# Weight blocks read into the place of their own low parts, a first operand made ahead, and two pools exchanged

## The chip, the cores and the metric

The kernel runs on one core of one Trainium2 chip. The time is device microseconds of one launch. In the core five engines work side by side, each through its own instructions in order: TensorE (PE) multiplies matrices, VectorE (DVE) and ScalarE (ACT) work element by element, GpSimd (POOL) does little here, and SyncE (SP) issues nearly all DMA transfers, one after another. Engines wait for each other through semaphores: an instruction that waits holds everything behind it on its engine.

## What is computed

Attention with a capped score, then two blocks of matrix products (shapes: 4 x 12 heads x 448 x 64, so 1792 tokens of 768; inner width 1024), all in float32:

```python
scores = cap * np.tanh(scale * np.matmul(q, k.transpose(0, 1, 3, 2)) / cap)
attn = softmax(scores)                       # with 1e-9 added to the sum
x = heads side by side of np.matmul(attn, v) # 1792 x 768
h = ((x @ w1) * (x @ w2)) @ w3 @ w_out       # first block, 1792 x 768
h = h @ w_in                                 # second block, 1792 x 1024
solu = h * softmax(h)
ln = (solu - mean) / np.sqrt(var + 1e-6) * g_ln
out = ln @ w_out2                            # 1792 x 768
```

`w3 @ w_out @ w_in` is multiplied into one matrix (`w_dr`) while attention runs, and `g_ln` is multiplied into the last matrix (`wg_dr`).

## The kernel before

A product of two float32 matrices is made of three matmuls (`THREE`): every operand is split into a high part (a cast to float32r, on ACT) and a low part (the rest, a subtraction on DVE). `split(th, tl, x)` does both, at lines 174 and 175, so the trace shows every split at these lines, under the name of the tile that is written.

Three stages follow each other. Attention runs with the products of the weights beside it. Then `gated()` makes `ab = (x @ w1) * (x @ w2)` for 16 steps of `f` (PE line 570; DVE multiplies at 578 into `abs`, and SP stores it to `ab_dr`). Beside it `ahead`, a list of loads and conversions, prepares what comes later. The last stage, which the change touches, multiplies by `w_dr` and by `wg_dr` in pairs of token tiles (128 tokens each, seven pairs). Both sides are cut 2 x 2, and seven products instead of eight are made of sums of the four pieces (`seven`, with operands numbered 1, 2, 6, 7, 5, 4, 3 in the order of use). For these products there are:

- weight blocks `ws[m]` (for `w_dr`) and `wg[m]` (for `wg_dr`), m = 1 to 7, each 128 x 4 x 512 (384 for `wg`) with a high and a low part. Blocks 5, 6, 7, 4 are sums that were made ahead and stored (`tw_dr`, `tg_dr`). `EARLY` blocks 1, 2, 6, 7, 5 of `ws` are loaded by `plan_block` during `gated()`, the `LATE` ones 4 and 3 at the start of the last stage. Every `wg[m]` takes the very place of `ws[m]`, once the last pair's product m has read it.
- operands `a[m]` of a pair (`operands`, or `turned_operands` for `wg`): pieces of the tokens and their sums `s1` to `s4`. The tokens come through landing buffers too: `ldab` (`load_ab`) and `ldc` (`load_c`), two tiles a pair.

There are three landing buffers (`LANDS`, tag `ld`) for all loads of this kind. In the kernel before, half a weight block (`part`) is read into a landing buffer (`landing`), split from there (`block_part`), and the buffer is then free for the next load.

Operands 1 and 2 of the first pair are made ahead of the stage (`first_operands`), in places of the pool `w3p`; operand 6 and the others are made by `operands(0)` after it. At the start of the last stage the pools of `gated()` are closed and `wsl` (late blocks), `hp` (sums, copies of products, `h`, `e`) and `op` (operands) are opened in their place, one behind another. A tile waits for whatever read or wrote its place before.

`solu` works on finished pairs of `h` (DVE and ACT) and stores `e` to `c_dr`. The last pair of `ws` (n = 6) has the first pair of `wg` following; `turned` transposes tokens on PE (line 760, `tp`). The order in which instructions of independent parts stand on an engine is made by a scheduler at build time, so the change also moves instructions that it doesn't name.

Of the kernel before, what the change touches and what calls it, by code (L numbers as in the profile page):

```python
# [10 lines left out]
F32 = mybir.dt.float32  # L11
F32R = mybir.dt.float32r
# [33 lines left out]
def raw(ap):  # L46

    return ap.bitcast(F32)
# [50 lines left out]
def attention_moe_solu(ctx: ExitStack, tc: tile.TileContext, q, k, v, cap, w12, w3t, wo, win, wout2, g_ln, out):  # L99
# [31 lines left out]
    def opened(stack, name, side="left"):  # L131
        cm = tc.tile_pool(name=name, bufs=1, side=side, reuse_waits="tile")
        stack.append(cm)
        return cm.__enter__()
# [15 lines left out]
    def landing(i, src, n, kind):  # L150
        t = conv.tile([P, 2 * HALF], U32, tag="ld", bufs=LANDS, name=f"ld{i}")
        lands[i] = t[:, :n].bitcast(kind)
        dst = lands[i]
        if len(src.shape) == 3:
            dst = dst.rearrange("p (a b) -> p a b", a=src.shape[1])
        elif len(src.shape) == 4:
            dst = dst.rearrange("p (a b c) -> p a b c", a=src.shape[1], b=src.shape[2])
            for g in range(src.shape[1]):
                sync.dma_start(out=dst[:, g], in_=src[:, g])
            return  # L160
        sync.dma_start(out=dst, in_=src)
# [11 lines left out]
    def split(th, tl, x):  # L173
        act.copy(th, x)
        dve.tensor_tensor(tl, x, raw(th), ALU.subtract)  # L175
# [301 lines left out]
    def block_src(m, part, dr, t_dr):  # L477

        two = slice(2 * part, 2 * part + 2)
        if m in (6, 7, 5, 4):  # L480
            return t_dr[(5, 6, 7, 4).index(m), :, two, :]
        g, h = {1: (0, 0), 2: (1, 0), 3: (1, 1)}[m]
        return dr[two, :, g, h, :].rearrange("i p n -> p i n")

    def block_part(i, dst, part):
        x = lands.pop(i)
        two = slice(2 * part, 2 * part + 2)
        split(dst[:, 0, two, :], dst[:, 1, two, :], x.rearrange("p (a n) -> p a n", a=2))

    def fifth(m):  # L490
        if m not in place["ws"]:
            close(right, 1)
            place["w5"] = opened(right, "ws5", "right")
            place["ws"][m] = place["w5"].tile([P, 2, NF // 2, HALF], F32R, tag=f"w{m}", name=f"ws{m}")
        return place["ws"][m]

    def plan_block(m, part):
        i = len(ahead.items)
        there = (lambda: "ws" in place) if m != EARLY[4] else (lambda: (NF + 5, PASSES[1][1]) in fin)
        ahead.add(("f", m, part), lambda: landing(i, block_src(m, part, W4, tw_dr), 2 * HALF, F32), lambda: None,  # L500
                  lambda: block_part(i, fifth(m), part), None, there)

    def plan_last(f):
        for u in range(2):
# [40 lines left out]
    def operand(a, m, x, name, p=None):  # L545
        a[m] = op.tile([P, 2, HALF], F32R, tag="op", bufs=NOP, name=f"{name}_{m}") if p is None else p
        split(a[m][:, 0], a[m][:, 1], x)
# [1 line left out]
    begun = {}  # L549

    def first_operands():
        x = lands["ab0"]
        for m, h in ((1, 0), (2, 1)):
            operand(begun, m, x[:, h * HALF:(h + 1) * HALF], "a0", w3p.tile([P, 2, HALF], F32R, tag="w3", bufs=W3, name=f"a0_{m}"))
    ahead.add("a0", lambda: load_ab(0), lambda: None, first_operands, None, lambda: (NF + 2, PASSES[1][0]) in fin)

    def gated():
# [119 lines left out]

    wsl, hp, op = opened(left, "wsl"), opened(left, "hp"), opened(left, "op")  # L680
    for m in LATE:
        ws[m] = wsl.tile([P, 2, NF // 2, HALF], F32R, tag=f"w{m}", name=f"ws{m}")
    ps_cm = tc.tile_pool(name="ps3", bufs=1, space=PSUM, reuse_waits="tile")
# [36 lines left out]
    def operands(n):  # L720

        x1, x2 = (lands.pop(f"ab{t}") for t in (2 * n, 2 * n + 1))
        a11, a12, a21, a22 = x1[:, :HALF], x1[:, HALF:], x2[:, :HALF], x2[:, HALF:]
        s1, s2, s3, s4 = (hp.tile([P, HALF], F32, tag="sm", bufs=4, name=f"s{i}_{n}") for i in range(4))
        a, name = (dict(begun) if n == 0 else {}), f"a{n}"
        if n:
            operand(a, 1, a11, name)
            operand(a, 2, a12, name)
        dve.tensor_tensor(s1, a21, a22, ALU.add)
        dve.tensor_tensor(s2, s1, a11, ALU.subtract)  # L730
        operand(a, 6, s2, name)
        dve.tensor_tensor(s3, a11, a21, ALU.subtract)
        operand(a, 7, s3, name)
        operand(a, 5, s1, name)
        operand(a, 4, a22, name)
        dve.tensor_tensor(s4, a12, s2, ALU.subtract)
        operand(a, 3, s4, name)
        return a
# [48 lines left out]
    def load_wg(m):  # L787
        wg[m] = (wsp if m in EARLY[:4] else place["w5"] if m in EARLY else wsl).tile([P, 2, NF // 2, HALF], F32R, tag=f"w{m}", name=f"wg{m}")[:, :, :, :w]
        for part in range(2):
            landing("wg", block_src(m, part, G4, tg_dr), 2 * w, F32)  # L790
            block_part("wg", wg[m], part)

    a = operands(0)
    for m in LATE:
        for part in range(2):
            landing("wl", block_src(m, part, W4, tw_dr), 2 * HALF, F32)
            block_part("wl", ws[m], part)
    load_ab(1)
    for n in range(PAIRS):
        tps, last = {}, n + 1 == PAIRS  # L800
        if last:
# [83 lines left out]
```

## Time and profile before

| | us |
|---|---|
| median of 3 runs | 857.79 (857.79 to 859.17) |
| the profiled execution | 857.35 |
| its span, first to last instruction | 854.4 |
| PE busy | 828.9 |
| DVE busy | 598.4 |
| ACT busy | 480.8 |

The span is what the trace's clock counts; 2.95 us of the profiled execution lie around it. PE is busy for 97% of it, with a matmul counted as busy until its modelled end, so that a running series of short ones overlaps.

### The profile page before, as it was taken

The page shows a single profiled execution, that of the slowest core. Times are in us where ns is not written, and L with a number is a line of the kernel's source. Part 1 is how long each engine was busy: PE and PEld are TensorE (multiplying, and loading weights), DVE is VectorE, ACT ScalarE, POOL GpSimd, SP SyncE. Part 2 cuts the span into 40 slices and gives each one's busy share as a digit, 9 for nine tenths or more (in the row PEclk, how much of TensorE's full clock was granted, in tenths as well). Part 3 has the DMA queues.
Part 4 walks back from the last instruction along what each step waited for, and adds up shares of the span by engine and source line. Part 5 has one row for each costly group of instructions (what it writes and reads, how often), then busy time and mean ns, then how long its engine had stood idle before and what let it go on. Part 6 is the DMA issues. An engine that isn't in the chain of part 4 may idle for free.

```text
span 854.4 us, 12340 instructions
## 1 busy us (share of the span) xinstructions
PE 828.9 (97%) x4392; PEld 687.7 (80%) x4392; DVE 598.4 (70%) x1068; ACT 480.8 (56%) x745; POOL 75.3 (9%) x147
## 2 busy tenths in 40 slices
PE   6999999999999999999989999999999999899998
PEld 4677998767677777777778899997788888799998
DVE  7999977887766587777874443444888877974452
ACT  5789538798777576767753112122465565653341
POOL 1011101111101111101101000000000000100000
PEclk8999999999999999999999999999999999899999
DMA  7886785686863376658769799793533234662211
GB/s 267 260 231 196 221 243 160 228 288 210 286 205 91 89 260 213 201 183 289 247 201 314 248 384 385 261 309 121 149 122 99 99 109 151 212 244 105 105 62 74
DMA packets 91549, 173.48 MB, mean 203 GB/s; under 512 B 9696, under 2 KB 61152, under 8 KB 89440
## 3 DMA queue, kind: packets, MB, share of 16 engines
q1 hardware_dynamic: 86496, 161.51, 56.8%
q0 software_dynamic: 4992, 11.19, 5.2%
q8 instruction: 34, 0.56, 0.3%
q14 instruction: 27, 0.22, 0.1%
HBM read 116.40 MB, written 50.68 MB: 196 GB/s over the span
## 4 chain that ended last, share of the span: by engine, by line
PE 45%; DMA 9%; DVE 6%; ACT 4%; issue 3%; POOL 0%; DVEq 0%; POOLq 0%; ACTq 0%
PE ab L570 18%; PE u L693 13%; PE v L693 6%; PE y L693 3%; DMA wg_dr<-cv 3%; PE o L271 2%; DMA rb<-r_dr 1%; PE tp L760 1%; DMA r_dr<-inv 1%; DMA wt<-w_dr 1%; ACT p L240 1%; DVE wg L175 1%; DMA ldwg<-wg_dr 1%; DVE cv L169 1%; DVE cv L170 1%
## 5 line engine op out<-in xcount | busy, mean ns | idle before, releaser
L570 PE MATMUL ab<-xs,wt 128*128 128x448 f32 x1152 | 249.0, 370 | 0.1
L570 PEld LDWEIGHTS ab<-xs,wt 128*128 128x128 f32 x1152 | 215.8, 189 | 27.6 <-issue 8.0
L239 ACT ACTIVATE sc<-sc,qscale 128x896 f32<-128x896 f32 x96 | 83.8, 885 | 34.7 <-PE sc L232 34.2
L271 PE MATMUL o<-hi,v 128*66 128x448 f32 (+1 forms) x396 | 94.4, 369 | 2.0 <-DVE hi L255 1.0
L240 ACT ACTIVATE p<-sc,capt 128x896 f32<-128x896 f32 x96 | 86.7, 920 | 1.1 <-PE o L271 0.3
L693 PE MATMUL u<-ws,a 128*128 128x512 f32 x336 | 81.2, 392 | 3.2 <-ACT u L697 2.0
L255 DVE TENSOR_TENSOR lo<-p,hi 128x896 fp32r<-128x896 f32 x66 | 71.5, 1084 | 13.9 <-ACT hi L251 13.7
L353 PEld LDWEIGHTS f<-w,w_o 128*128 128x128 f32 x576 | 72.6, 191 | 7.9 <-issue 4.1
L353 PE MATMUL f<-w,w_o 128*128 128x256 f32 x576 | 77.8, 288 | 0.0
L693 PEld LDWEIGHTS u<-ws,a 128*128 128x128 f32 x336 | 62.8, 188 | 17.4 <-ACT u L697 2.4
L371 PE MATMUL f<-w_i,w 128*128 128x512 f32 x288 | 74.7, 398 | 1.0 <-DVE w L175 1.0
L693 PE MATMUL u<-wg,c 128*128 128x384 f32 x336 | 66.7, 343 | 1.7 <-DVE wg L175 1.0
L371 PEld LDWEIGHTS f<-w_i,w 128*128 128x128 f32 x288 | 52.8, 188 | 17.2 <-issue 4.0
L271 PEld LDWEIGHTS o<-hi,v 128*66 128x66 f32 (+1 forms) x396 | 44.3, 135 | 24.7 <-DVE hi L255 3.2
L251 ACT CAST hi<-p 128x896 fp32r<-128x896 f32 x66 | 62.6, 950 | 0.5 <-PE o L271 0.4
L693 PEld LDWEIGHTS u<-wg,c 128*128 128x128 f32 x336 | 58.9, 190 | 3.4 <-DVE wg L175 1.8
L574 ACT COPY a<-ab 128x448 f32<-128x448 f32 x32 | 17.1, 533 | 76.1 <-PE ab L570 68.3
L168 DVE TENSOR_SCALAR cv<-ld 128x512 uint32<-128x512 uint32 (+1 forms) x80 | 32.5, 409 | 32.3 <-DMA wg_dr<-cv 13.6
L169 DVE SCALAR_TENSOR_TENSOR cv<-ld,cv 128x512 uint32<-128x512 uint32 (+1 forms) x80 | 52.0, 657 | 0.6
L170 DVE SCALAR_TENSOR_TENSOR cv<-ld,cv 128x512 uint32<-128x512 uint32 (+1 forms) x80 | 51.9, 658 | 0.5
L282 POOL DMA_DIRECT2D xr<-x x48 | 25.6, 535 | 280.4 <-ACT x L281 280.4
L271 PE MATMUL o<-lo,v 128*66 128x448 f32 x132 | 47.4, 365 | 1.1 <-DVE lo L255 1.1
(129 smaller groups left out, 1234.8 us busy)
## 6 DMA issues: line engine op xcount, KB each, us to landing
ld<-in_w SPq DMA_DIRECT2D x24, 512.0 KB, 4.5
w_dr<-wt SPq DMA_DIRECT2D x8, 1536.0 KB, 7.4
wt<-w_dr SPq DMA_DIRECT2D x8, 1536.0 KB, 7.7
ld<-in_w3t SPq DMA_DIRECT2D x16, 512.0 KB, 4.2
ab_dr<-abs SPq DMA_DIRECT2D x32, 224.0 KB, 4.9
ldab<-ab_dr SPq DMA_DIRECT2D x14, 512.0 KB, 3.9
c_dr<-e SPq DMA_DIRECT2D x14, 512.0 KB, 2.8
ldc<-c_dr SPq DMA_DIRECT2D x14, 512.0 KB, 4.4
```

The costliest lines, as they stand in the source:

```text
L168: dve.tensor_scalar(x, hi, 5, 2, ALU.logical_shift_left, ALU.logical_shift_right)
L169: dve.scalar_tensor_tensor(x, hi, 0xC0000000, x, ALU.bitwise_and, ALU.bitwise_or)
L170: dve.scalar_tensor_tensor(x, lo, 29, x, ALU.logical_shift_right, ALU.bitwise_or)
L239: act.activation(sc[:, :w, :S], sc[:, :w, :S], AF.Tanh, scale=qscale)
L240: act.activation(p, sc[:, :w, :S], AF.Exp, scale=capt)
L251: act.copy(hi, p)
L255: dve.tensor_tensor(lo, p, raw(hi), ALU.subtract)
L271: pe.matmul(outs[n, j][:v_.shape[-1], :S], v_, t[rows, j if c < 3 else 0], **flags)
L353: pe.matmul(f[:, :QW], lw[:, a], rw[:, e], start=(g == 0 and m == 0), stop=(g == NF - 1 and m == 2))
L371: pe.matmul(f, w34[:, a, c, :], rw[:, e], start=(c == 0 and m == 0), stop=(c == NC - 1 and m == 2))
L570: pe.matmul(pp[f, b, i][:, :S], w[:, u], xs[b, c][:, e], start=(c == 0 and m == 0), stop=(c == NC - 1 and m == 2))
L693: pe.matmul(bank, a[m][:, x, k * P:(k + 1) * P], wb[m][:, e, k, :], start=(first and k == 0 and i == 0), stop=(k == NF // 2 - 1 and i == 2 ...
```

## The change

A weight block is read by DMA straight into the place of its low part; the split then casts from there into the high part and subtracts in place. `block_load` and `block_split` take the place of `landing` and `block_part`, for early and late `ws` blocks and for `wg`. The two half blocks of a `wg` are loaded one behind the other and then split. Block 5's load stands behind the last sums for `tg_dr`, since its place is opened at the load now. The four loads of late blocks and the second pair's tokens are issued in the code ahead of `operands(0)`. `first_operands` also makes `s1`, `s2` (in the two buffers of tag `cv`) and operand 6 of the first pair. `op` is opened ahead of `hp`.

```diff
@@ -482,10 +482,12 @@
         g, h = {1: (0, 0), 2: (1, 0), 3: (1, 1)}[m]
         return dr[two, :, g, h, :].rearrange("i p n -> p i n")
 
-    def block_part(i, dst, part):
-        x = lands.pop(i)
-        two = slice(2 * part, 2 * part + 2)
-        split(dst[:, 0, two, :], dst[:, 1, two, :], x.rearrange("p (a n) -> p a n", a=2))
+    def block_load(m, part, dr, t_dr, dst):
+        sync.dma_start(out=raw(dst[:, 1, 2 * part:2 * part + 2, :]), in_=block_src(m, part, dr, t_dr))
+
+    def block_split(dst, part):
+        hi, lo = (dst[:, i, 2 * part:2 * part + 2, :] for i in range(2))
+        split(hi, lo, raw(lo))
 
     def fifth(m):
         if m not in place["ws"]:
@@ -495,10 +497,9 @@
         return place["ws"][m]
 
     def plan_block(m, part):
-        i = len(ahead.items)
-        there = (lambda: "ws" in place) if m != EARLY[4] else (lambda: (NF + 5, PASSES[1][1]) in fin)
-        ahead.add(("f", m, part), lambda: landing(i, block_src(m, part, W4, tw_dr), 2 * HALF, F32), lambda: None,
-                  lambda: block_part(i, fifth(m), part), None, there)
+        there = (lambda: "ws" in place) if m != EARLY[4] else (lambda: (NF + 5, PASSES[1][1]) in fin and ("tg", NF // 2 - 1, 1) in ahead.done)
+        ahead.add(("f", m, part), lambda: block_load(m, part, W4, tw_dr, fifth(m)), lambda: None,
+                  lambda: block_split(ws[m], part), None, there)
 
     def plan_last(f):
         for u in range(2):
@@ -549,9 +550,17 @@
     begun = {}
 
     def first_operands():
-        x = lands["ab0"]
-        for m, h in ((1, 0), (2, 1)):
-            operand(begun, m, x[:, h * HALF:(h + 1) * HALF], "a0", w3p.tile([P, 2, HALF], F32R, tag="w3", bufs=W3, name=f"a0_{m}"))
+        x1, x2 = lands["ab0"], lands["ab1"]
+        s1, s2 = first_sums = [conv.tile([P, HALF], U32, tag="cv", bufs=2, name=f"s{i}_0").bitcast(F32) for i in (1, 2)]
+        begun["sums"] = first_sums
+
+        def begin(m, x):
+            operand(begun, m, x, "a0", w3p.tile([P, 2, HALF], F32R, tag="w3", bufs=W3, name=f"a0_{m}"))
+        begin(1, x1[:, :HALF])
+        begin(2, x1[:, HALF:])
+        dve.tensor_tensor(s1, x2[:, :HALF], x2[:, HALF:], ALU.add)
+        dve.tensor_tensor(s2, s1, x1[:, :HALF], ALU.subtract)
+        begin(6, s2)
     ahead.add("a0", lambda: load_ab(0), lambda: None, first_operands, None, lambda: (NF + 2, PASSES[1][0]) in fin)
 
     def gated():
@@ -677,7 +686,7 @@
 
 
 
-    wsl, hp, op = opened(left, "wsl"), opened(left, "hp"), opened(left, "op")
+    wsl, op, hp = opened(left, "wsl"), opened(left, "op"), opened(left, "hp")
     for m in LATE:
         ws[m] = wsl.tile([P, 2, NF // 2, HALF], F32R, tag=f"w{m}", name=f"ws{m}")
     ps_cm = tc.tile_pool(name="ps3", bufs=1, space=PSUM, reuse_waits="tile")
@@ -721,14 +730,17 @@
 
         x1, x2 = (lands.pop(f"ab{t}") for t in (2 * n, 2 * n + 1))
         a11, a12, a21, a22 = x1[:, :HALF], x1[:, HALF:], x2[:, :HALF], x2[:, HALF:]
-        s1, s2, s3, s4 = (hp.tile([P, HALF], F32, tag="sm", bufs=4, name=f"s{i}_{n}") for i in range(4))
+        s3, s4 = (hp.tile([P, HALF], F32, tag="sm", bufs=4, name=f"s{i}_{n}") for i in (3, 4))
         a, name = (dict(begun) if n == 0 else {}), f"a{n}"
         if n:
+            s1, s2 = (hp.tile([P, HALF], F32, tag="sm", bufs=4, name=f"s{i}_{n}") for i in (1, 2))
             operand(a, 1, a11, name)
             operand(a, 2, a12, name)
-        dve.tensor_tensor(s1, a21, a22, ALU.add)
-        dve.tensor_tensor(s2, s1, a11, ALU.subtract)
-        operand(a, 6, s2, name)
+            dve.tensor_tensor(s1, a21, a22, ALU.add)
+            dve.tensor_tensor(s2, s1, a11, ALU.subtract)
+            operand(a, 6, s2, name)
+        else:
+            s1, s2 = a.pop("sums")
         dve.tensor_tensor(s3, a11, a21, ALU.subtract)
         operand(a, 7, s3, name)
         operand(a, 5, s1, name)
@@ -787,15 +799,18 @@
     def load_wg(m):
         wg[m] = (wsp if m in EARLY[:4] else place["w5"] if m in EARLY else wsl).tile([P, 2, NF // 2, HALF], F32R, tag=f"w{m}", name=f"wg{m}")[:, :, :, :w]
         for part in range(2):
-            landing("wg", block_src(m, part, G4, tg_dr), 2 * w, F32)
-            block_part("wg", wg[m], part)
-
+            block_load(m, part, G4, tg_dr, wg[m])
+        for part in range(2):
+            block_split(wg[m], part)
+
+    for m in LATE:
+        for part in range(2):
+            block_load(m, part, W4, tw_dr, ws[m])
+    load_ab(1)
     a = operands(0)
     for m in LATE:
         for part in range(2):
-            landing("wl", block_src(m, part, W4, tw_dr), 2 * HALF, F32)
-            block_part("wl", ws[m], part)
-    load_ab(1)
+            block_split(ws[m], part)
     for n in range(PAIRS):
         tps, last = {}, n + 1 == PAIRS
         if last:
```

Two places are shown as they stand on the engines; the number behind the last `_` of a name is only a running one, and the number behind `a_` is that of the operand.

First ACT at the start of the last stage, before: `p_0` and `u_0` are copies of finished products of pair 0, `a_...` casts of operands, `ws_6144` and `ws_6145` late blocks.

```order
L174 CAST ws_6144<-ldwl 128x1024
L697 COPY p_0_6209<-u_6194 128x512
L174 CAST a_6_6155<-s_0_6150 128x512
L174 CAST a_7_6159<-s_0_6151 128x512
L174 CAST a_5_6162<-s_0_6149 128x512
L174 CAST a_4_6165<-ldab_5964 128x512
L174 CAST a_3_6169<-s_0_6152 128x512
L174 CAST ws_6144<-ldwl 128x1024
L174 CAST ws_6145<-ldwl 128x1024 x2
L697 COPY u_0_6236<-u_6194 128x512
```

And in the changed kernel:

```order
L706 COPY p_0_6195<-u_6180 128x512
L174 CAST a_7_6157<-s_0_6154 128x512
L174 CAST a_5_6160<-s_0_6017 128x512
L174 CAST a_4_6163<-ldab_5968 128x512
L174 CAST a_3_6167<-s_0_6155 128x512
L706 COPY u_0_6222<-u_6180 128x512
L174 CAST a_1_6281<-ldab_6150 128x512
L174 CAST a_2_6284<-ldab_6150 128x512
L174 CAST a_6_6289<-s_1_6280 128x512
L174 CAST ws_6141<-ws_6141 128x1024
L174 CAST a_7_6293<-s_1_6277 128x512
L174 CAST a_5_6296<-s_1_6279 128x512
```

The cast of operand 6 is gone from here, the copy `u_0` stands ahead of all late blocks, and these stand among the next pair's operands.

DVE at the same place, from the last product of `ab` on, before (`s_0` and `s_1` are sums of pair 0 and pair 1, `ldab_5962` and `ldab_5964` the tokens of pair 0, `h_6192` is a result of pair 0):

```order
L578 TENSOR_TENSOR abs_3_6127<-ab_15_3_6108,a_3_6106 128x448
L729 TENSOR_TENSOR s_0_6149<-ldab_5964 128x512
L730 TENSOR_TENSOR s_0_6150<-s_0_6149,ldab_5962 128x512
L732 TENSOR_TENSOR s_0_6151<-ldab_5962,ldab_5964 128x512
L175 TENSOR_TENSOR ws_6144<-ldwl,ws_6144 128x1024
L736 TENSOR_TENSOR s_0_6152<-ldab_5962,s_0_6150 128x512
L704 TENSOR_TENSOR h_6192<-y_6195,p_0_6209 128x512
L175 TENSOR_TENSOR a_6_6155<-s_0_6150,a_6_6155 128x512
L175 TENSOR_TENSOR a_7_6159<-s_0_6151,a_7_6159 128x512
L175 TENSOR_TENSOR a_5_6162<-s_0_6149,a_5_6162 128x512
```

And in the changed kernel, where `ldab_6150` and `ldab_6152` are the tokens of pair 1:

```order
L587 TENSOR_TENSOR abs_3_6124<-ab_15_3_6105,a_3_6103 128x448
L744 TENSOR_TENSOR s_0_6154<-ldab_5966,ldab_5968 128x512
L748 TENSOR_TENSOR s_0_6155<-ldab_5966,s_0_6018 128x512
L713 TENSOR_TENSOR h_6178<-y_6181,p_0_6195 128x512
L739 TENSOR_TENSOR s_1_6279<-ldab_6152 128x512
L740 TENSOR_TENSOR s_1_6280<-s_1_6279,ldab_6150 128x512
L175 TENSOR_TENSOR a_7_6157<-s_0_6154,a_7_6157 128x512
L175 TENSOR_TENSOR a_5_6160<-s_0_6017,a_5_6160 128x512
L744 TENSOR_TENSOR s_1_6277<-ldab_6150,ldab_6152 128x512
```

The sums `s1`, `s2` and operand 6 of pair 0 are gone from here, and two sums of pair 1 stand ahead of the low part of operand 7.

Then SP at the passage to `wg`, before (`ldwg` are landing buffers, `c_dr<-e` stores of `solu`):

```order
L161 DMA ldwg<-wg_dr 128x2x384
L753 DMA c_dr<-e_6957 128x1024
L753 DMA c_dr<-e_6970 128x1024
L161 DMA ldwg<-wg_dr 128x2x384 x3
L161 DMA ldwg<-tg_dr 128x768 x3
L753 DMA c_dr<-e_7111 128x1024
L161 DMA ldwg<-tg_dr 128x768 x2
L753 DMA c_dr<-e_7124 128x1024
L161 DMA ldwg<-tg_dr 128x768 x3
L161 DMA ldwg<-wg_dr 128x2x384 x2
```

And in the changed kernel (`wg_7245` is block 1, then 2, 6, 7, 5, 4, 3):

```order
L486 DMA wg_7245<-wg_dr 128x2x384 x2
L486 DMA wg_7283<-wg_dr 128x2x384 x2
L486 DMA wg_7290<-tg_dr 128x2x384 x2
L486 DMA wg_7297<-tg_dr 128x2x384 x2
L161 DMA ldc_7327<-c_dr 128x1024
L161 DMA ldc_7507<-c_dr 128x1024
L486 DMA wg_7304<-tg_dr 128x2x384 x2
L486 DMA wg_7311<-tg_dr 128x2x384 x2
L486 DMA wg_7318<-wg_dr 128x2x384 x2
L161 DMA ldc_7509<-c_dr 128x1024
L765 DMA c_dr<-e_7097 128x1024
L765 DMA c_dr<-e_7110 128x1024
```

The loads go in pairs to the blocks themselves, with loads of `ldc` among them and the stores of `e` behind them.

Between them on PE in the changed kernel, from the last read of `ws` block 1 (`ws_5065`) to the first of `wg` block 1 (`wg_7245`):

```order
L702 MATMUL u_7128<-ws_5065,a_1_7071 128x512 x4
L702 MATMUL y_7129<-ws_5066,a_2_7074 128x512 x4
L702 MATMUL u_6970<-ws_6142,a_3_6935 128x512 x12
L702 MATMUL y_7129<-ws_5066,a_2_7074 128x512 x3
L772 MATMUL tp_0_7158<-ident,ldc_7122 128x128 x4
L702 MATMUL u_7128<-ws_5067,a_6_7079 128x512 x12
L772 MATMUL tp_1_7177<-ident,ldc_7124 128x128 x4
L702 MATMUL v_7130<-ws_5068,a_7_7083 128x512 x12
L772 MATMUL tp_2_7196<-ident,ldc_7122 128x128 x4
L772 MATMUL tp_3_7214<-ident,ldc_7124 128x128 x4
L702 MATMUL u_7331<-wg_7245,c_1_7256 128x384 x7
```

Between the two stand products 2, 3, 6 and 7 of pairs 5 and 6, and 16 transposes.

## Rows read from the trace of the kernel before

**Rows 1.** What PE waited for, 560 us to the end: us in total, times, longest.
```profile
PE u L693 <- ACT u L697: 2.0, 1, 2.0
PE tp L760 <- DMA ldc<-c_dr: 1.5, 1, 1.5
PE u L693 <- ACT a L174: 1.2, 1, 1.2
PE u L693 <- DVE wg L175: 1.0, 2, 0.9
PE u L693 <- ACT wg L174: 0.6, 1, 0.6
PE v L693 <- DVE wg L175: 0.6, 1, 0.6
```

**Rows 2.** Timeline of PE, 588 to 622: start, us, engine, line, operation, [idle before].
```profile
588.40 2.96 PE L693 MATMUL u<-ws,a 128*128 128x512 f32 x12
...
603.18 3.47 PE L693 MATMUL u<-ws,a 128*128 128x512 f32 x14 [2.03 <-ACT u L697]
...
617.06 2.88 PE L693 MATMUL u<-ws,a 128*128 128x512 f32 x12
619.78 2.88 PE L693 MATMUL v<-ws,a 128*128 128x512 f32 x12
```

**Rows 3.** Timeline of ACT in the same stretch.
```profile
594.20 0.58 ACT L697 COPY p<-u 128x512 f32<-128x512 f32 x1 [4.55 <-PE y L693]
...
601.60 1.04 ACT L174 CAST ws<-ldwl 128x1024 fp32r<-128x1024 f32 x1 [2.31 <-DMA ldwl<-w_dr]
602.55 0.58 ACT L697 COPY u<-u 128x512 f32<-128x512 f32 x1
```

**Rows 4.** Timeline of PE, 734 to the end.
```profile
734.96 1.47 PE L693 MATMUL v<-wg,c 128*128 128x384 f32 x7
...
753.68 2.36 PE L693 MATMUL u<-wg,c 128*128 128x384 f32 x12
...
774.35 0.60 PE L760 MATMUL tp<-ident,ldc 128*128 128x128 f32 x4
774.70 0.60 PE L693 MATMUL u<-wg,c 128*128 128x384 f32 x2
...
846.20 2.24 PE L693 MATMUL v<-wg,c 128*128 128x384 f32 x12
848.27 2.25 PE L693 MATMUL u<-wg,c 128*128 128x384 f32 x12
```

**Rows 5.** Windows: busy PE, PEld, DVE, ACT, POOL; PEclk, DMA share, GB/s.
```profile
742.00:750.00 8.00, 7.16 (x24) 5.85 (x24) 7.16 (x17) 5.12 (x8) 0.55 (x1) 0.57 0.65 210
720.00:740.00 20.00, 18.93 (x97) 16.52 (x95) 19.55 (x34) 14.84 (x25) 3.75 (x2) 1.00 0.69 219
740.00:760.00 20.00, 17.22 (x83) 15.01 (x84) 16.16 (x33) 12.89 (x23) 1.10 (x2) 0.83 0.76 268
```

**Rows 6.** What ACT waited for, 715 to 755.
```profile
ACT wg L174 <- DMA ldwg<-tg_dr: 4.8, 3, 2.5
```

**Rows 7.** What the DMA queue (SP) waited for, 440 us to the end.
```profile
SPq L161 <- DVE wg L175: 13.7, 10, 4.0
```

**Rows 8.** Tile `ldwg`, a landing buffer for `wg` half blocks.
```profile
DMA to landing us min/median/max: 3.1/3.5/5.4
```

**Rows 9.** Groups by line and shape: count, busy us, mean ns of one, idle before.
```profile
L175 DVE TENSOR_TENSOR a<-s,a 128x512 fp32r<-128x512 f32 x28 | 18.6, 683 | 0.3 <-ACT a L174 0.3
...
L175 DVE TENSOR_TENSOR wg<-ldwg,wg 128x768 fp32r<-128x768 f32 x14 | 13.1, 950 | 3.2 <-ACT wg L174 3.2
...
L174 ACT CAST wg<-ldwg 128x768 fp32r<-128x768 f32 x14 | 11.7, 836 | 15.2 <-DMA ldwg<-wg_dr 10.1 <-DMA ldwg<-tg_dr 4.8
```

**Rows 10.** Timeline of DVE at the last `ab` product's end.
```profile
588.65 0.62 DVE L578 TENSOR_TENSOR abs<-ab,a 128x448 f32<-128x448 f32 x1 [6.82 <-PE ab L570]
```

**Rows 11.** Tile `ldab`, a landing buffer for `ab` tiles.
```profile
DMA to landing us min/median/max: 3.7/3.9/6.3
```

## Prediction

> **What bounds the kernel now.** I read the page first: its busy times say that TensorE (PE) is busy nearly all the time, so time can only come out of places where it waits or runs slowly. The table of PE's waits from 560 us to the end names six, 6.9 us together [rows 1]; in the span they lie in two places, and nowhere else in the last 290 us. The first is the start of the last stage, where products of 448 columns (`ab`) give way to the seven-product pairs; the second is the passage from the last pair of `ws` products to the first pairs of `wg` products.
>
> How much each place loses is better read from the PE timeline than from the named waits, since a matmul after a break is drawn longer than its place in a running series.
>
> First place [rows 2]: from 588.40 to 603.18 PE works through four products of 12 matmuls (rows with x2 and x10 lie between). In a running series a product takes 619.78 - 617.06 = 2.72 us. Four take 10.9; 14.8 passed, so 3.9 us are lost. Two waits, 1.2 and 2.0 us [rows 1], are most of it. Both go through ScalarE (ACT) [rows 3]. The copy `p` of the first product ends its idle time only at 594.20, when product `y`, which it doesn't read, is done: its buffer lies in the pool `hp`, over the place of operand `a0_2`, which `y` still reads. The cast of the sixth operand is queued behind `p`. Later the copy `u` at 602.55 is queued behind casts of `ws` blocks, the last of which began at 601.60, when its block had come.
>
> Second place [rows 4]: from 734.96 to 753.68, 18.72 us, PE does 48 matmuls of 384 columns (the x7, x1, x5, ... rows) and 16 transposes. Running, 12 such matmuls take 848.27 - 846.20 = 2.07 us and four transposes 774.70 - 774.35 = 0.35: 8.3 + 1.4 = 9.7 us. So 9.0 us are lost. Named waits are 3.7 of them (1.5 + 1.0 + 0.6 + 0.6, [rows 1]). In 742 to 750 the granted clock is 0.57, mostly the lower of its two levels (1.2 of 2.4 GHz), so PE, busy 7.16 us, did the work of 4.1: another 3.1 [rows 5]. Ahead of it stood a cluster of short idles; in 720 to 740 the clock is 1.00. The remaining 2.2 are restarts after breaks. Their cause is the landing buffers: a `wg` half block must land in one of three, be split by ACT and VectorE (DVE), and only then can the next load be issued. ACT waits 4.8 us for the loads from `tg_dr` alone [rows 6], and the queue waits 13.7 us in 10 places for DVE's splits [rows 7].
>
> **The change, part by part.**
>
> *`wg` blocks into place.* The same 14 loads, 14 casts and 14 subtractions; none is added. Gone is the wait for a landing buffer; instead each load waits until PE has read the old block of that number for the last time. Tightest is block 1. After its last read PE still has 43 matmuls of 512 columns and 16 transposes until it first wants `wg` block 1 (the PE rows of the change): 43 x 2.72/12 + 1.4 = 11.1 us. The new chain is a landing of 3.5 us (3.1 to 5.4, [rows 8]), a cast of 0.84 and a subtraction of 0.95 for the first half [rows 9], the second half about a cast later: some 6.2 us, 8.1 with the longest landing. So it fits, unless ACT and DVE are 3 us behind. The queue waits at the head for PE now, but what stands behind (loads for later pairs, stores of `e`) is wanted a pair later. The landings freed let the `ldc` loads go earlier, which takes the 1.5 us wait of the transposes too. Gain between 3.7 (named waits only) and 9.0; I take 9.0 less a residue, below.
>
> *Late `ws` blocks into place.* These four loads now start after PE's last `ab` matmul at 588.6 and one more load, instead of one before it and three behind split after split. PE wants the first after five products and most of two, some 18 us later; four landings one behind another take less. Their casts now stand behind the copy `u` in ACT's queue, so the 2.0 us wait goes. ACT's copy `u` instead waits for the last stores of `ab`, the last of them issued behind the sum of 588.65 [rows 10], some 7 us before PE ends the product with the sixth operand (588.4 + 3 x 2.72 = 596.6). I cost that at nothing.
>
> *Sixth operand ahead, operands' pool in front.* Two sums, one cast and one subtraction move ahead of the last `ab` product, where DVE and ACT have idle time; PE is the cover there. With `op` in front, `p` no longer lies over `a0_2`. The 1.2 us wait goes. What is late next: the seventh operand. Its low part stands on DVE behind the first sum of the next pair, which needs the fourth `ab` tile. That load is issued when DVE has done the last `abs` (588.65 + 0.62, [rows 10]) and two sums of 0.68 [rows 9]: 590.6. It lands 3.9 us later, 3.7 to 6.3 [rows 11]: 594.5, at worst 596.9. DVE gets there after `h`, at about 594.9 (the first two products take 5.6 us, and 0.7 for `h`), and needs two sums and the subtraction, 2.0 us: 596.9. PE wants it after three products and two matmuls: 588.4 + 8.2 + 0.4 = 597.0. So nothing is lost in the middle case, 1.9 us with the longest landing. I take nothing, because the queue is nearly empty there.
>
> *Early blocks into place.* Five more blocks, spread over 480 to 580 us. PE has no named wait from 560 to 588 [rows 1] and each block is wanted after 588; the loads of `wt` are pushed back behind them in the queue by some microseconds, with more than that in hand. Nothing gained; a loss there is in the range's upper end.
>
> *Sum.* 3.9 + 9.0 = 12.9 us, less 0.2 because the first two products ran at 2.8 us rather than 2.72 with nothing waiting. Against it stands DVE: it is busy 19.55 of 20 us in 720 to 740 [rows 5], and that stretch is to be followed without a pause. I leave 0.6 us there and 0.1 elsewhere. The profiled execution took 857.35 us (the median shown is 857.79, 0.05% more): 857.35 - 12.0 = **845.4 us**. With the named waits alone, 6.9, it would be 850.5; with all of it, 844.5.
>
> **A rule that speaks against it.** The trace shows loads that are ready before PE wants them wherever landing buffers exist in number, and the wait only where three are too few [rows 6, 7]. The Trainium skill ("Trainium Kernel Development and Optimization", Best Practices) says to double-buffer, so that DMA and compute overlap; reading a block straight into the place that PE still reads gives up one buffer. If that decides, this is the fourth rival below, priced from rows.
>
> **Rivals.**
> 1. *The seventh operand waits for the fourth `ab` tile.* For: only 0.1 us in hand, and a longest landing of 6.3 [rows 11]. Against: the median. 1.9 us: 847.3.
> 2. *DVE becomes the bound at the second place.* If none of its work leaves 720 to 760, where it is busy some 35.7 us (19.55 + 16.16, [rows 5]), then 31 us of PE work don't hold it: 4.7 us come back, and if these idles bring the lower clock again, its 3.1 as well: 850 to 853. For: 98% busy. Against: it has idle time in the 20 us to either side, and a third of its work there is `solu`, which PE wants only pairs later.
> 3. *Nothing comes of it*: the waits return a product later, since DMA brings the blocks no faster. 856 to 859. For: ACT's waits name DMA [rows 6]. Against: the loads themselves last 3.5 us [rows 8], and the queue waited for buffers [rows 7].
> 4. *Slower: the load into place starts too late.* Block 1's chain is 6.2 us against 11.1. Every microsecond beyond 11.1 is a stall at each of seven blocks. To lose the 12 us as well as its own, a chain would have to last 11.1 + 12/7 = 12.8 us, twice as long; then 858 to 866. For: ACT and DVE serve their queues in order, and a cast that waits for its block holds copies that PE wants. Against: the durations.
>
> **How the numbers follow.** Forecast 0.68 (own range 844.3 to 847.2), rival 1 0.07, rival 2 0.13, rival 3 0.05, rival 4 0.07. 0.2% (1.7 us) is about what a measurement can tell from no change. Faster: forecast and rivals 1 and 2, 0.88; same 0.05, slower 0.07. The range, 843.8 to 852.5, holds the forecast, rival 1 and most of rival 2, with 0.6 us below for the spread of runs.
>
> **What would show it.** In the changed profile: PE without a wait on ACT between the fourth and fifth product of the last stage; `p` copied right behind its product; the stretch from the first `wg` matmul on at clock 1.00 and without waits on `wg`; no wait of transposes on `ldc`. The step on rival 1 is wrong if PE waits on DVE two matmuls into the first product on `v`; the residue is wrong if waits on DVE's `c` or `wg` add up to over 2 us. The whole is wrong if PE's wait on a `wg` cast is ended by its DMA.

## The result, and the profile after

The changed kernel takes 844.9 us (median of 4 runs, 839.33 to 848.07) against 857.79 of the kernel before: ratio 0.985, interval 0.9806 to 0.9894. Run again it took 842.93 us, ratio 0.9857 (0.9833 to 0.988). Forecast were 845.4 us. The medians are of the fast runs; one timed run of `all_moved` below (852.35 us) was slow and is left out.

The total agrees more closely than the parts. The span of the profile splits where PE starts the first product of the last stage: **the last stage** went from 854.4 - 588.40 = 266.0 us [rows 2] to 837.6 - 582.09 = 255.5 us. That is 10.5 us, where 12.0 were forecast. The other microseconds lie ahead of it, where the instructions of attention stand in the same order as before; they are taken up below.

PE's waits from 560 us to the end, the table that had six rows before [rows 1], is now only a heading:

```profile
core 0 of [0], span 837.6 us
engine line waited for: us in total, times, longest us
```

First place, PE (start, us, engine, line, operation): four products in 593.29 - 582.09 = 11.20 us, where 14.78 passed [rows 2].

```profile
582.09 2.96 PE L702 MATMUL u<-ws,a 128*128 128x512 f32 x12
584.89 2.96 PE L702 MATMUL y<-ws,a 128*128 128x512 f32 x12
587.69 2.96 PE L702 MATMUL u<-ws,a 128*128 128x512 f32 x12
590.49 2.96 PE L702 MATMUL v<-ws,a 128*128 128x512 f32 x12
593.29 3.43 PE L702 MATMUL u<-ws,a 128*128 128x512 f32 x14
```

On ACT the copy `p` follows its own product at once (before it waited for `y`, [rows 3]), and the copy `u` follows the third product:

```profile
585.09 0.59 ACT L706 COPY p<-u 128x512 f32<-128x512 f32 x1 [5.94 <-PE u L702]
...
590.69 0.59 ACT L706 COPY u<-u 128x512 f32<-128x512 f32 x1 [2.18 <-PE u L702]
```

Second place, windows (busy PE, PEld, DVE, ACT, POOL; PEclk, DMA share, GB/s), which answer to [rows 5]: PE busy all the time at clock 1.00, while DVE has no pause in the first window.

```profile
720.00:740.00 20.00, 20.00 (x120) 19.31 (x119) 20.00 (x36) 14.23 (x25) 1.06 (x2) 1.00 0.62 207
740.00:760.00 20.00, 20.00 (x122) 19.82 (x122) 16.38 (x31) 10.68 (x21) 1.53 (x2) 1.00 0.45 165
```

So nothing waits any more, and still 1.5 us are missing. The rows that show them are the first ones: a running product on an early block takes 2.80 us, as 610.01 to 612.81 to 615.61 below, where 2.72 was read in the kernel before [rows 2]. On the late blocks 4 and 3 it takes 2.74 to 2.75 (2.76 before).

```profile
610.01 2.96 PE L702 MATMUL y<-ws,a 128*128 128x512 f32 x12
612.81 2.96 PE L702 MATMUL v<-ws,a 128*128 128x512 f32 x12
615.61 5.29 PE L702 MATMUL u<-ws,a 128*128 128x512 f32 x22
```

### The profile page after: what moved, and what is told of

It is laid out like the page before. It is cut to its first block, busy times and chain, and to the rows that moved or that the text cites. A ratio compares the mean times of both kernels' runs of the same rounds, so it can differ in the third digit from the quotient of the medians.

```text
span 837.6 us, 12351 instructions
## 1 busy us (share of the span) xinstructions
PE 822.7 (98%) x4392; PEld 684.9 (82%) x4392; DVE 597.3 (71%) x1068; ACT 480.9 (57%) x745; POOL 73.8 (9%) x147
## 4 chain that ended last, share of the span: by engine, by line
PE 52%; DMA 6%; DVE 4%; ACT 3%; issue 2%; POOL 0%; DVEq 0%; POOLq 0%; ACTq 0%
PE ab L579 19%; PE u L702 16%; PE v L702 8%; PE y L702 4%; DMA wg_dr<-cv 3%; PE o L271 2%; PE tp L772 1%; DMA rb<-r_dr 1%; ACT p L240 1%; DMA r_dr<-inv 1%; DVE cv L169 1%; DVE cv L170 1%; PE sc L232 1%; DVE cv L168 1%; ACT wt L174 0%
## 5 line engine op out<-in xcount | busy, mean ns | idle before, releaser
L239 ACT ACTIVATE sc<-sc,qscale 128x896 f32<-128x896 f32 x96 | 83.8, 886 | 35.9 <-PE sc L232 35.4
L240 ACT ACTIVATE p<-sc,capt 128x896 f32<-128x896 f32 x96 | 86.8, 921 | 1.1 <-PE o L271 0.3
```

The lines of the kernel that those rows point to most:

```text
L239: act.activation(sc[:, :w, :S], sc[:, :w, :S], AF.Tanh, scale=qscale)
L240: act.activation(p, sc[:, :w, :S], AF.Exp, scale=capt)
```

## The experiments

Theory: the gain of the last stage is 3.9 us of the first place and 9.0 of the second, from the edits to which the prediction put them, and a slower pace takes some back. Rivals: the edits act otherwise, and the pace belongs to one execution. All runs in one table: start and length of the last stage in the profiled execution, the length up to the first `wg` matmul and from there on, then the timed runs. Each ratio is to the kernel before as timed in the same round, whose median was 856.84 to 857.79 us. The length is the sharper measure: in three profiles with the same instructions in the last stage (changed, again, early_landed) it repeats to 0.1 us, while timed runs of one kernel differ by up to 13. It isn't that sharp between different kernels: behind the first `wg` matmul, runs that change nothing there still differ from the kernel before by 0.3 to 1.1 us.

| run | starts at | last stage | up to `wg` | from `wg` on | median | ratio to before, interval |
|---|---|---|---|---|---|---|
| before | 588.4 | 266.0 | 131.9 | 134.1 | 857.79 | |
| changed | 582.1 | 255.5 | 129.8 | 125.7 | 844.9 | 0.985 (0.9806 to 0.9894) |
| again | 583.7 | 255.5 | 129.8 | 125.7 | 842.93 | 0.9857 (0.9833 to 0.988) |
| early_landed | 586.9 | 255.5 | 129.8 | 125.7 | 846.02 | 0.9868 (0.9829 to 0.9908) |
| op_moved | 586.5 | 253.6 | 128.2 | 125.3 | 844.04 | 0.986 (0.9836 to 0.9883) |
| all_moved | 588.5 | 252.0 | 126.9 | 125.0 | 842.84 | 0.9835 (0.9794 to 0.9876) |
| last_moved | 589.8 | 252.3 | 127.2 | 125.1 | 843.73 | 0.983 (0.9785 to 0.9874) |
| wg_landed | 588.9 | 263.1 | 129.8 | 133.2 | 853.83 | 0.9967 (0.9949 to 0.9986) |
| wg_only | 593.9 | 257.5 | 132.0 | 125.5 | 849.72 | 0.9922 (0.9895 to 0.995) |
| lands_rb | 585.5 | 261.7 | 132.0 | 129.7 | 852.52 | 0.9934 (0.9906 to 0.9963) |
| pools_moved | 587.3 | 263.3 | 129.6 | 133.7 | 852.88 | 0.9941 (0.9908 to 0.9973) |
| sixth_moved | 588.2 | 262.5 | 128.1 | 134.4 | 853.28 | 0.995 (0.9919 to 0.998) |
| late_only | 590.3 | 268.4 | 133.3 | 135.2 | 857.47 | 1.0007 (0.9977 to 1.0036) |
| before_moved | 588.1 | 269.9 | 135.2 | 134.7 | 857.3 | 0.9997 (0.997 to 1.0024) |

**The pace.** First the changed kernel unaltered, then with its operands moved.

> The changed kernel once more, nothing altered. Last stage is counted from the start of its first product on PE to the end of the span: 255.5 us in the first profile (266.0 in the kernel before). Theory A, what differs between executions lies ahead of the last stage: the last stage takes 255.5 us within 0.3, its running products of 512 columns stay at 2.80 us each, and only the time at which it starts (582.1) differs, by some microseconds. Theory B, the pace of 2.80 us (2.72 in the kernel before) belongs to that one execution: it comes out nearer 2.72 here and the last stage near 253.

255.5 us and 2.80 us a product again: the pace belongs to the kernel, only the start moves.

In the built program the operands' pool began at byte 109024 of a partition before, at 69920 after. Modulo 512 that is 480 and 288.

```diff
-    wsl, op, hp = opened(left, "wsl"), opened(left, "op"), opened(left, "hp")
+    wsl, pad = opened(left, "wsl"), opened(left, "pad")
+    pad.tile([P, 48], F32, name="pad")
+    op, hp = opened(left, "op"), opened(left, "hp")
```

> The changed kernel with the operands' pool and all behind it 192 bytes further on in SBUF, which gives the operands the place modulo 512 bytes that they had before the change. Theory A, the pace of a 512-column matmul hangs on the place of what it reads modulo some power of two: products go from 2.80 to 2.72 us (2.76 for blocks 4 and 3, which stay), the last stage from 255.5 to about 252.5. Theory B, it hangs on the half of SBUF in which the operands lie, or on the traffic of other engines: 2.80 stays, 255.5 stays.

Moved by 192 bytes, still in the lower part, running products take 2.72 us again (block 7, 616.95 to 619.67), those of blocks 4 and 3 2.76. The last stage takes 1.9 us less.

```profile
616.95 2.88 PE L704 MATMUL v<-ws,a 128*128 128x512 f32 x12
619.67 5.15 PE L704 MATMUL u<-ws,a 128*128 128x512 f32 x22
```

The reverse, in the kernel before:

```diff
-    wsl, hp, op = opened(left, "wsl"), opened(left, "hp"), opened(left, "op")
+    wsl, hp, pad = opened(left, "wsl"), opened(left, "hp"), opened(left, "pad")
+    pad.tile([P, 80], F32, name="pad")
+    op = opened(left, "op")
```

> The kernel before with the operands' pool alone 320 bytes further on (its operands then lie modulo 512 bytes where the changed kernel has them, but in the same part of SBUF as before). If the place modulo a power of two sets the pace, running products of 512 columns go from 2.72 to 2.80 us and the last stage from 266.0 to some 268; if only the part of SBUF counted, 2.72 and 266.0 stay.

2.80 appears where 2.72 was, in the upper part too, as in the last row:

```profile
603.03 5.08 PE L695 MATMUL u<-ws,a 128*128 128x512 f32 x14 [2.10 <-ACT u L699]
607.95 0.63 PE L695 MATMUL y<-ws,a 128*128 128x512 f32 x2
...
618.55 2.96 PE L695 MATMUL u<-ws,a 128*128 128x512 f32 x12
621.35 0.86 PE L695 MATMUL v<-ws,a 128*128 128x512 f32 x3
```

The last stage is 3.9 us longer, more than the 2 expected. 1.6 of it is another thing: the 14 matmuls from 603.03 take 4.92 us, in the kernel before 3.30 (from 603.18, [rows 2]). After the wait of 2.10 us they ran partly at the lower clock, 0.66 on average (busy PE, PEclk, DMA share, GB/s):

```profile
603.00:608.00 5.00, 4.97 (x15) 0.66 0.79 218
```

Another 0.7 us lie behind the first `wg` matmul, where products of 384 columns keep their pace. So the place costs some 1.6 us here.

The part of SBUF is excluded as the cause. That it is the place modulo some power of two fits all four places tried. Which power isn't known: shifts of 192 and 320 bytes don't tell 128 from 256 or 512.

More was moved in two runs. Everything on the left side of SBUF (a `pad` tile of 192 bytes behind `ident`):

> The changed kernel with 192 bytes left free ahead of all pools on the left side, so that operands, late blocks, converted weights and ab's tokens all move. If the place sets the pace of every 512-column matmul: the last stage 253.6 (operands alone moved) less 0.6 for late blocks and 0.2 for the first operands, 252.8 us; the 288 matmuls of 512 columns beside attention 2 us less if they are on the path. If it sets that of 448 columns too (1152 matmuls of ab at 203 ns), ab's running pace falls below 203 ns and the time by up to 7 us more; if only 512 columns are touched, 203 ns stay.

Last stage 252.0, its products of 512 columns at 2.72 from the second on. The tail of `ab` took 130.7 us instead of 128.9 and 129.3 in the two profiles of the changed kernel. It is one series of 632 matmuls of 448 columns, without a wait:

```profile
457.84 130.86 PE L580 MATMUL ab<-xs,wt 128*128 128x448 f32 x632
```

From 457.84 to the last stage at 588.53 that is 206.8 ns for each, against 203.9 and 204.7 in the changed kernel. So 448 columns didn't gain by the move. I then moved the last stage alone:

```diff
-    wsl, op, hp = opened(left, "wsl"), opened(left, "op"), opened(left, "hp")
+    pad, wsl, op, hp = (opened(left, i) for i in ("pad", "wsl", "op", "hp"))
+    pad.tile([P, 48], F32, name="pad")
```

> The changed kernel with 192 bytes left free ahead of the last stage's pools alone, so that late blocks and operands move and the weights and tokens of ab stay. If the two effects seen are separate, the last stage takes 252.0 us as with everything moved, plus 0.2 for the first three products, whose operands stay: 252.2; and ab's tail from the end of attention to the last stage takes 129.4 us again, not the 130.7 of everything moved. It should be the fastest of all, about 3 us under the changed kernel, which the timed runs can hardly tell from spread.

The last stage came as expected, 252.3. The tail of `ab` did not: 131.2 us though nothing of `ab` had moved (130.9 in early_landed too). Here the cause is another one than in all_moved. PE waits once for a converted weight that is loaded back, first in last_moved, then in early_landed:

```profile
PE ab L579 <- DMA wt<-w_dr: 1.7, 1, 1.7
PE ab L585 <- DMA wt<-w_dr: 1.4, 1, 1.4
```

The changed kernel has no such wait in either profile; lands_rb (1.4) and wg_only (1.6) have it, with the early blocks through landing buffers. What makes that load late in some executions stays open. In the last stage this version beats the changed kernel by 3.2 us; its timed runs can't show that (0.983 against 0.985, intervals as wide as 0.009).

**The second place.** `wg` alone changed back, and alone changed:

```diff
-            block_load(m, part, G4, tg_dr, wg[m])
-        for part in range(2):
-            block_split(wg[m], part)
+            landing("wg", block_src(m, part, G4, tg_dr), 2 * w, F32)
+            two = slice(2 * part, 2 * part + 2)
+            split(wg[m][:, 0, two, :], wg[m][:, 1, two, :], lands.pop("wg").rearrange("p (a n) -> p a n", a=2))
```

> The changed kernel with the wg half blocks through the landing buffers again, the rest as changed. Theory of the prediction, all 9.0 us lost at the second place come from that: waits on wg casts and subtractions, a stretch of granted clock near half, and a wait of the transposes are back, the last stage takes some 264.5 us. Rival, part of the 9.0 came from elsewhere (the order on ACT and DVE, the freed loads of late blocks): 258 to 262.

263.1: 7.6 us come back. PE's waits, and the window from 740 to 750 us, with a granted clock of 0.66 (columns as in the windows above). The first wait is put down to `st`, but a `wg` subtraction on DVE had ended only 0.06 us before PE went on at 742.76.

```profile
PE v L702 <- DVE st L760: 2.1, 1, 2.1
PE u L702 <- DVE wg L175: 0.6, 1, 0.6
PE v L702 <- DVE wg L175: 0.4, 1, 0.4
PE u L702 <- ACT wg L174: 0.3, 1, 0.3
```

```profile
740.00:750.00 10.00, 7.77 (x30) 7.30 (x30) 8.25 (x17) 5.49 (x9) 1.53 (x2) 0.66 0.74 258
```

Of the 9.0 us the transposes' wait for `ldc` (1.5, [rows 1]) did not return.

The kernel before with `block_load` and `block_split` for `wg` alone (the reverse of this diff):

> The kernel before with the wg blocks alone read into place. Theory of the prediction: the second place gains 9.0 us by itself, the granted clock stays at 1.00 from 720 us on, the first place still loses its 3.9, the last stage takes 266.0 - 9.0 = 257.0 us. Rival, DVE becomes the bound there: PE waits on DVE's c or wg, the last stage takes 259 to 262. As to the pace: operands lie where they did before, so running products take 2.72 us.

257.5: 8.5 us. The two waits of the first place stand, those of the second are gone, and PE has no pause at clock 1.00 (busy PE, PEclk, DMA share, GB/s):

```profile
PE u L700 <- ACT u L704: 2.0, 1, 2.0
PE u L700 <- ACT a L174: 1.2, 1, 1.2
```

```profile
740.00:760.00 20.00, 20.00 (x124) 1.00 0.51 177
```

Is it the number of buffers? The kernel before with a fourth one, in attention's buffer `rb`:

```diff
+    wgs = [0]
+
+    def landing_wg(src, n):
+        wgs[0] += 1
+        if wgs[0] % 4:
+            landing("wg", src, n, F32)
+            return
+        t = conv.tile([P, 2, S], F32, tag="rb", name=f"rbwg{wgs[0]}").rearrange("p a s -> p (a s)")[:, :n]
+        lands["wg"] = t
+        sync.dma_start(out=t.rearrange("p (a b) -> p a b", a=2), in_=src)
...
-            landing("wg", block_src(m, part, G4, tg_dr), 2 * w, F32)
+            landing_wg(block_src(m, part, G4, tg_dr), 2 * w)
```

> The kernel before with a fourth landing buffer for wg half blocks: every fourth of the 14 goes through a buffer of attention that is free by then. Theory of the prediction, the second place is slow because three buffers are too few: with a fourth the waits on wg shrink and the half clock with them, the last stage takes 259 to 262 us without any load into place. Rival, the landing through a buffer as such (its chain of cast, subtraction, next load) or the rate of DMA is the limit: 265 to 266.

261.7: one buffer more gives 4.3 us, the clock stays at 1.00 from 720 to 760, and of the `wg` waits one is left. The wait for `ldc` is the larger now. Most of the 4.3 is the clock: from 740 to 760 PE is busy for 17.86 us at 1.00, in the kernel before for 17.22 at 0.83 [rows 5], some 2.9 us of work less. The timed runs agree: their mean granted clock is 0.990 to 0.994, that of the kernel before in the same round 0.984 to 0.990.

```profile
PE u L693 <- ACT u L697: 2.1, 1, 2.1
PE tp L760 <- DMA ldc<-c_dr: 1.9, 2, 1.5
PE u L693 <- ACT a L174: 1.2, 1, 1.2
PE v L693 <- DVE wg L175: 0.8, 1, 0.8
```

**The first place.** In these runs `pad` keeps the old pace. The kernel before with `op` in front alone (the lines added in op_moved's diff):

> The kernel before with the operands' pool in front of the sums' pool (192 bytes on, so that the pace is that of before) and nothing else; the sixth operand is made where it was. If the place of the copy p over an operand still read is the root of both waits of the first place, the last stage takes some 262.5 us as with the sixth operand made ahead. If the sixth operand has to be made ahead as well, a wait of about 1 us on its cast or its low part remains: 263.5 to 265.

263.3: 2.7 us less, 2.3 of them ahead of the first `wg` matmul. What PE still waits for there:

```profile
PE u L695 <- DVE a L175: 0.5, 1, 0.5
PE u L695 <- ACT a L174: 0.4, 1, 0.4
```

With `first_operands` and `operands` as in the changed kernel in addition:

> The kernel before with the first pair's sixth operand made ahead and the operands' pool in front (192 bytes moved, so that the pace is that of before); late blocks and wg through landing buffers as before. Theory of the prediction, the two waits of the first place are separate: the 1.2 us wait on the cast of a_6 goes, the 2.0 us wait on the copy u stays, the last stage takes 266.0 - 1.2 = 264.8 us. Rival, the late blocks' landing sets the time of that copy: PE comes earlier to the same point and waits 3.2 us there, the last stage stays at 266.0.

262.5: ahead of the first `wg` matmul 3.8 us less than before, 1.5 more than by the pools alone (the total hides it, since the part behind is 0.6 us longer than in pools_moved). Both waits are gone (PE goes from 593.78 to 602.05 without one), with late blocks still through landing buffers. In the order built, `u` stands behind two late casts, no longer four, and these were done:

```profile
594.51 2.00 ACT L174 CAST ws<-ldwl 128x1024 fp32r<-128x1024 f32 x2
596.78 0.59 ACT L707 COPY u<-u 128x512 f32<-128x512 f32 x1 [0.28 <-PE u L703]
```

The sixth operand ahead without the pools' exchange was not tried.

Late blocks alone:

```diff
...
+    for m in LATE:
+        for part in range(2):
+            block_load(m, part, W4, tw_dr, ws[m])
+    load_ab(1)
     a = operands(0)
     for m in LATE:
         for part in range(2):
-            landing("wl", block_src(m, part, W4, tw_dr), 2 * HALF, F32)
-            block_part("wl", ws[m], part)
-    load_ab(1)
+            block_split(ws[m], part)
```

> The kernel before with the late blocks alone read into place (and loaded ahead of the first operands in the code); in the order built the copy u still stands behind all late casts on ACT. Theory of the prediction, the copy u must stand ahead of the late casts, and the loads into place end soon enough: with u behind them, PE waits for the fourth landing, and something between 0 and 2.0 us of the 2.0 us wait is left; last stage 264 to 266. Rival, loads that can start only after the last ab product make that wait longer: over 266.

268.4, 2.4 us longer: 1.4 ahead of the first `wg` matmul, 1.1 behind it. The first part doesn't come from the landings. PE:

```profile
593.07 2.96 PE L700 MATMUL y<-ws,a 128*128 128x512 f32 x12
598.69 0.73 PE L700 MATMUL u<-ws,a 128*128 128x512 f32 x2 [2.65 <-ACT a L174]
599.84 4.10 PE L700 MATMUL u<-ws,a 128*128 128x512 f32 x10 [0.42 <-DVE a L175]
603.78 2.89 PE L700 MATMUL v<-ws,a 128*128 128x512 f32 x12
```

and DVE, where `h` now stands ahead of the second sum (L737), which the sixth operand needs:

```profile
591.07 0.68 DVE L736 TENSOR_TENSOR s<-ldab 128x512 f32<-128x512 f32 x1
596.69 0.69 DVE L711 TENSOR_TENSOR h<-y,p 128x512 f32<-128x512 f32 x1 [4.94 <-ACT p L704]
597.30 0.68 DVE L737 TENSOR_TENSOR s<-s,ldab 128x512 f32<-128x512 f32 x1
```

`h` waits for the copy `p`, `p` for product `y`. The wait on the operand's cast grew from 1.2 to 2.65 us, and after it ten matmuls took 3.94 us instead of 2.3: the lower clock again (0.72 in the mean of 598 to 604). The wait for `u` is gone. Neither theory had this: the order of DVE decided. In the second part, which wasn't edited, PE waits longer for a cast of `wg` (0.6 in the kernel before, [rows 1]); why is open.

```profile
PE u L700 <- ACT wg L174: 2.1, 1, 2.1
```

**Ahead of the last stage.** The changed kernel with `plan_block` and `block_part` of before for the early blocks:

> The changed kernel with the five early blocks through the landing buffers again. Theory of the prediction, early blocks read into place gain nothing: the last stage stays at 255.5 us, ab's tail at 129 us, and the time is that of the changed kernel within the spread. Rival, part of the time that the changed kernel gained ahead of the last stage comes from them: ab's tail or the start of the last stage is later than in both profiles of the changed kernel (582.1, 583.7) by over 3 us, and the timed median above 846.

The last stage stays at 255.5. The signs named for the rival did appear (start 586.9, tail of `ab` 130.9, median 846.02), but they don't single out these loads: op_moved, all_moved and last_moved have the early blocks in place and start at 586.5 to 589.8, and the longer tail here is the wait for `wt` that last_moved has too.

## Why the prediction was right, and where it was not

**The second place** was sized right: 9.0 us less 0.6 forecast, 8.5 measured with `wg` alone. The mechanism is shown from three sides: taken back it costs 7.6, a fourth landing buffer gives 4.3 of it, mostly by the clock, and the granted clock is 1.00 in both runs without these waits.

**The chain of block 1** took 9.4 us, not 6.2. The queue (SP), ACT and DVE rows of the changed kernel:

```profile
700.43 5.25 SPq L486 DMA_DIRECT2D wg<-wg_dr  x4
```

```profile
704.31 0.83 ACT L174 CAST wg<-wg 128x768 fp32r<-128x768 f32 x1 [3.29 <-DMA wg<-wg_dr]
```

```profile
705.18 0.96 DVE L175 TENSOR_TENSOR wg<-wg 128x768 fp32r<-128x768 f32 x1 [4.98 <-ACT wg L174]
706.05 2.34 DVE L755 TENSOR_REDUCE st<-h 128x1 f32<-128x1024 f32 x2
...
708.91 0.95 DVE L175 TENSOR_TENSOR wg<-wg 128x768 fp32r<-128x768 f32 x1
```

The second half's subtraction ends at 709.86, since DVE did `solu`'s two reductions (2.34 us) and `h` between. PE starts with the block at 711.91, 11.5 us after the load's issue (11.1 forecast). So 2.1 us were left where I had counted 4.9. Rival 4 is refuted, but on block 1 it came nearer than the sum of the bare durations said: what stands in DVE's queue belongs into such a chain. The rule that it leaned on (the Trainium skill, "Trainium Kernel Development and Optimization", Best Practices: double-buffer so that DMA and compute overlap) holds in the trace as far as a fourth landing buffer gained 4.3 us; reading into the one place gained 8.5, since PE's own 11 us of other products cover the load.

**DVE as the bound** (rival 2) didn't come: busy 20.00 of 20 us and yet PE waited for nothing. The work that could wait moved on: PE does in 30.7 us from its first `wg` matmul what took 39.7 before, and DVE does 30.7 us of work in that time, not 35.4. The residue left for it, 0.6, is about what wg_only shows (0.5).

**The seventh operand** (rival 1) came as worked out. The fourth `ab` tile was issued 2.1 us after the stage's start (2.2 forecast), DVE took it up 6.5 us after (6.5), PE started product `v` after 8.4 (8.2) and didn't wait.

**The first place** has the right size, 3.6 us of 3.7, by the wrong edits. The step that failed is that the two waits are separate, 1.2 us for the sixth operand and the pools, 2.0 us for the late blocks ("so the 2.0 us wait goes"). Up to the first `wg` matmul the pools alone gave 2.3, with the sixth operand it was 3.8, the whole, and the late blocks alone lose 1.4. In the two runs that gain, `p` is early, the operands' casts go early, and `u` has only two late casts in front of it in the built order, four before. With the late blocks alone `u` stayed behind all late casts, so what they give with `u` ahead of them and nothing else changed isn't known; they weren't needed.

**A term is missing**: the pace. I took 2.72 us for a running product from the kernel before and counted the pools' exchange by its waits only. It also moved the operands, and at their new place a product on an early block takes 2.80: 255.5 - 253.6 = 1.9 us. A row of the prediction held the sign of it: the first two products ran at 2.8 us "with nothing waiting". Their operands lie in `w3p`, which begins at byte 61728, also 288 modulo 512, and in all_moved, which shifts `w3p` too, the second product takes 2.72. The sum of the last stage then is 131.9 - 129.8 = 2.1 us up to the first `wg` matmul (3.8 as in sixth_moved, less 1.7 of the pace) and 134.1 - 125.7 = 8.4 from there on: the 10.5 measured. Without the pace it is 266.0 - 253.6 = 12.4, where 12.0 were forecast.

**That the total came out at 844.9** rests on the part ahead. The medians differ by 12.9, the last stages by 10.5. Over the 14 profiles the last stage starts between 582.1 and 593.9 us, and it doesn't follow the edits: wg_only, whose attention is that of the kernel before, starts 5.5 us later than it. Taking the last stage from the median, 857.79 - 266.0 = 591.8 stand against 844.9 - 255.5 = 589.4 and, run again, 587.4; the other runs lie between 587.4 (before_moved) and 592.2 (wg_only). So I don't ascribe the 2.4 us to the change. By its own sum, with the pace, the forecast would have been about 847; that it came within 0.5 us of the median is chance.

## What to carry to other kernels

A landing buffer is a queue of its own: when loads wait for it, count how long the final place stands free before it is wanted, and load there. When a pool is moved, count what it overlies and what the matmuls' own rows do at the new address, and compare one running product before and after; 192 bytes of padding were worth 3.2 us of the last stage here. When a wait goes, look at the built order of the engine that released it: here the edits of the first place each moved a copy or a sum to another place in the queue, and one of them alone made things worse.

## What the runs showed of the hardware that was not expected

- A running matmul of 512 columns in this kernel takes 227 ns (2.72 / 12) to 233 (2.80 / 12), by the place of its operands in SBUF: 2.72 us where operands and blocks both lie at 480 modulo 512, 2.80 with operands at 288 and blocks at 480, 2.76 with operands at 480 and blocks at 288, 2.74 to 2.75 with both at 288. Products of 384 columns took 2.07 to 2.09 in all these runs. Matmuls of 448 columns vary by something else as well: the 632 of `ab`'s tail took 203.9 and 204.7 ns each in two executions of the changed kernel, and leaving waits out 204.6 in the kernel before and 202.0 in wg_only, where they read the same addresses.
- A wait of the same length is followed by the lower clock or not. After 2.10 us in before_moved the clock fell to 0.66 (above). In lands_rb, at the same place and after the same 2.10 us, it stayed at 1.00:

```profile
600.34 3.49 PE L693 MATMUL u<-ws,a 128*128 128x512 f32 x14 [2.10 <-ACT u L697]
```

```profile
600.00:604.00 4.00, 3.66 (x16) 1.00 1.05 292
```

The length of one idle time alone doesn't tell it, then. The same kind of difference lies in attention, in the same order of instructions, at PE's wait for `p` (L240) near 440 us. The kernel before waits 1.87 us there, and the clock of the next 4 us is 0.57:

```profile
444.56 0.47 PE L228 MATMUL sc<-qh,kh 128*128 128x448 f32 x1 [1.87 <-ACT p L240]
...
445.27 3.95 PE L570 MATMUL ab<-xs,wt 128*128 128x448 f32 x11
```

```profile
445.00:449.00 4.00, 4.00 (x14) 0.57 0.94 346
```

In the changed kernel the wait is 1.36 us, the clock stays at 1.00, and the same 11 matmuls of `ab` are drawn with 2.39 us, not 3.95:

```profile
440.60 0.47 PE L228 MATMUL sc<-qh,kh 128*128 128x448 f32 x1 [1.36 <-ACT p L240]
...
441.31 2.39 PE L579 MATMUL ab<-xs,wt 128*128 128x448 f32 x11
```

Of the 14 profiles, 13 have a wait at this place. After 1.13 to 1.36 us (three of them) the clock stayed at 1.00. After 1.60 to 1.89 us it fell in eight, to 0.50 to 0.70 over the next 4 us, and stayed at 1.00 in two (1.84 in before_moved, 1.88 in all_moved). Such a step of 1.6 us can shift the start of the last stage; what makes the wait longer or shorter was not tried.
